# Attention weights turned by vector-engine blocks and DMAs, in place of tensor-engine transposes, for the last eight head pairs

## The chip, the cores and the metric

The kernel runs on one core of a Trainium2 chip. The metric is the device time of one execution in microseconds (us). The engines are TensorE (PE; its weight loads are listed as PEld), VectorE (DVE), ScalarE (ACT), GpSimd (POOL) and SyncE (SP). SP computes nothing here; it issues all the DMAs of the kernel before. Every engine works through its own queue in order, and semaphores tie the queues together.

## The reference, cut to what matters

Four batches of 576 tokens, 8 heads of width 64, all in float32. Three parts follow one another:

```
attention  out_d   = softmax(q_d k_d^T / 8) v_d      q_d, k_d, v_d: means over groups of 4 tokens
           out_loc = softmax(mask(q k^T / 8)) v      mask: |i - j| < 4
           x       = repeat(out_d, 4) + out_loc
block 1    x = x + relu(layernorm(x) w_ch1) w_ch2            512 -> 2048 -> 512
block 2    u = x + (token mixing over 576 -> 256 -> 576 with relu)
           out = u + relu(u w_ch1') w_ch2'                   512 -> 1536 -> 512
```

The change touches the local attention alone (`out_loc`), between the exponential of its scores and their product with v.

## The kernel before, in words

**Attention by pairs.** 4 batches of 4 pairs of heads make 16 pairs, numbered 0 to 15. For a pair, the local scores are computed in 9 blocks of 64 queries against a band of 70 keys (`KW`), which lie in 5 tiles of 128 queries (`NTL`). The steps are functions of the code: `s_pe` (L265 on) computes scores and mask into two PSUM banks, one per head; `s_max` (DVE) takes the row maximum; `s_exp` (L294 on, the ACT instruction is L300) writes the exponentials to the SBUF tile `sm`, with queries on the partitions. `t_pe` (L363) turns each of the 10 tiles (2 heads x 5) by a PE transpose, 128 queries x 70 keys to 70 keys x 128 queries, in three groups that take one PSUM bank each (4, 4 and 2 tiles). `t_copy` (L370) copies each group on ACT to the SBUF tile `et`, with keys on the partitions. `av_pe` (L468) multiplies `et` with v, and `av_norm` divides by the row sum (for pairs 4 to 15 ten small ACT instructions, L502). The coarse attention of the pair (`q_sums`, `d_pe`, `d_max`, `d_exp`, `td_pe`, `td_copy`, `avd_pe`, `avd_norm`) runs beside it, goes through a scratch in HBM (`up_write` L428, `up_read` L439 and L443) and is added into `x` by `av_add` (POOL, L515). `sm` and `et` have one buffer each for pairs 5 to 15, so the transposes of pair n must have read `sm` before pair n+1 writes it, and `av_pe` of pair n-1 must have read `et` before pair n fills it.

**Block 1 and 2 by units.** Tokens go in 9 chunks of 256. A unit is one chunk with 128 hidden columns: `g1` (L629, 12 matmuls of 256 columns into a PSUM bank of `h`), then relu and a split into a high and a low part, on ACT (L635, high) and DVE (L636, low), into `ht`, then `g2` (L650, 6 matmuls of 512 columns that accumulate the chunk's output). There are 16 units a chunk in block 1 and 12 in block 2, 252 in all. In the program's order, `g1` of unit i+1 stands ahead of `g2` of unit i. Weights of block 1 arrive by SP in 32 pieces of 512 KB (`load_unit`, L190). The last 28 of them pass through the staging tile `st` (`stage`, L140 on, 3 buffers of 1024 words a partition); five steps turn a piece to two float32r parts: three on DVE (L149, L154, L159), one on ACT (L164), one on DVE (L167). At most three pieces are loaded and not yet converted.

**The order of work.** Pairs 0 to 4 follow a list written out by hand (`START`). From there each step gets a position in the row of units (`put`): the pairs' steps are spread by `LATER` over units 1 to 25, 26 to 51 and 52 to 82, one step every 1.0 to 1.4 units, in the order `a_scores(n)`, `a_values_down(n-1)`, `a_down(n)`, `a_values(n-1)`, `a_turn(n)`, `a_turn_down(n)`. `a_scores(8)` has position 20.2, `a_down(8)` 22.6, `a_values(7)` 23.8 and `a_turn(8)` 26; one piece of weights is split in each of the units 0 to 27, and three ahead of it is loaded. A scheduler of the compiler then places the instructions by a plan of time; the position is an instruction's priority in it. The queue of each engine is fixed when the kernel is built.

**A turn of the same kind that is there already.** For chunks 3 to 17, the normalized or mixed tokens are turned by `xt_turn`: a DVE instruction transposes each 32x32 block of 128x512 in place (L579), and 16 DMAs of 16 KB, issued by SP (L586), bring each block row to its partitions in runs of 128 bytes.

Of the kernel before, what the change touches and what calls it, by code (L numbers as in the profile page):

```python
# [7 lines left out]
F32 = mybir.dt.float32  # L8
F32R = mybir.dt.float32r
I32 = mybir.dt.int32  # L10
ACTF = mybir.ActivationFunctionType
# [15 lines left out]
KW = 70  # L27
NTL = 5
# [11 lines left out]
SETS = 3  # L40

EARLY = 2

START = """
    q_sums 0; s_pe 0; s_max 0; fill; d_pe 0; q_sums 1; s_exp 0; d_max 0; fill; fill; fill; v_sums 0;
# [46 lines left out]
def block_kernel(ctx: ExitStack, tc: tile.TileContext, qk, vw, vg, g_ln, wa, t1, t2, wb, band, out):  # L92
    nc = tc.nc
    UA = wa.shape[0]
    UB = wb.shape[0]
    scale = 1.0 / float(D) ** 0.5
# [28 lines left out]
    def psg(tag=None):  # L125
        if tag is None:
            turn[0] += 1
            tag = rota[turn[0] % len(rota)]
        return POOLS[tag].tile([128, 512], F32, tag=tag, name=tag)
# [10 lines left out]
    def stage(n):  # L140
        return sp["pool"].tile([128, 2 * QW], I32, tag="st", name="st", bufs=sp["n"])[:, :2 * n]
# [36 lines left out]
    def load_unit(i, part, gate=None):  # L178
        w, m = (wa, i) if i < UA else (wb, i - UA)
        if i < EARLY:  # L180
            if part == 0:
# [39 lines left out]
    def buf(n, tag):  # L221
        if n == SETS and tag == "qk":
            return extra[-1][tag]
        if n < START_PAIRS and n % SETS:
            return extra[n % SETS - 1][tag]
        return at.tile([128, WORDS[tag]], F32, tag=tag, name=tag, bufs=1)
# [3 lines left out]
    def att_load(n, tag):  # L230
        if n < len(order):
            b, p = order[n]
            src = {"qk": qk, "vw": vw, "vg": vg}[tag][b, p]
            t = buf(n, tag)
            nc.sync.dma_start(out=t[:src.shape[0]], in_=src)
            ld[n, tag] = t
# [10 lines left out]
    sts = {}  # L247
# [45 lines left out]

    def s_exp(n):  # L294
        nm = nms[n]
        sm = sts[n]["sm"] = buf(n, "sm").rearrange("p (h t k) -> p h t k", h=2, t=NTL)
        pss = pending.pop((n, "s"))
        for h in range(2):
            for tl in range(NTL):
                nc.scalar.activation(  # L300
                    out=sm[:, h, tl], in_=pss[h][:, tl], func=ACTF.Exp, scale=scale, bias=nm[:, h, tl]
                )

    def a_scores(n):
        for f in (q_sums, s_pe, s_max, s_exp):
            f(n)

    def d_pe(n, tag=None):
        qkd = sts[n].pop("qkd")
        pss = []  # L310
        for h in range(2):
            ps = psg(tag)
            psv = ps[:HG, :2 * SG].rearrange("q (c k) -> q c k", c=2)
            pss.append(psv)
        for c in range(2):
            for h in range(2):
                d = slice(64 * h, 64 * h + 64)
                nc.tensor.matmul(  # L318
                    out=pss[h][:, c, :], lhsT=qkd[d, 0, c * HG:(c + 1) * HG], rhs=qkd[d, 1, :],
                    start=True, stop=True,  # L320
                )
        ld.pop((n, "qk"))
        pending[n, "d"] = pss
# [17 lines left out]
    def v_sums(n):  # L341
        vgt = ld[n, "vg"][:HG].rearrange("p (c n) -> p c n", c=2)
        vd = sts[n]["vd"] = vgt[:, :, :130].rearrange("p c (h d) -> p c h d", h=2)
        for t in range(3):
# [3 lines left out]
                in1=vgt[:, :, o:o + 128].rearrange("p c (h d) -> p c h d", h=2), op=ALU.add,  # L348
            )

    def a_down(n):
        d_pe(n)
        att_load(ahead(n), "qk")
        for f in (d_max, d_exp, v_sums):
            f(n)
# [171 lines left out]
    def ahead(n):  # L527
        return n + 1 if n >= START_PAIRS else len(order)
# [246 lines left out]
    def put(pos, f, *args):  # L775
        u, half = divmod(int(2 * pos), 2)
        u = min(u, NSEQ - 1)
        (bg if half else mid)[u].append(lambda: f(*args))
# [84 lines left out]
    def conv_step(k):  # L863
# [5 lines left out]

    steps = {f.__name__: f for f in (  # L870
        q_sums, v_sums, s_max, s_exp, d_max, d_exp, t_pe, t_copy, td_pe, td_copy, avd_pe, avd_norm, up_write,
        up_read, av_pe, av_norm, load, fill, consts, ln_center, xt_pe, xt_hi, xt_lo,
    )}
# [4 lines left out]
    with tc.manual_schedule():  # L878
# [17 lines left out]
        rota[:] = ["acc", "g"]  # L896
        nl[0] = nsp[0] = EARLY * NPC
        for step in START.split(";"):
# [15 lines left out]
    for n in range(START_PAIRS, len(order) + 1):  # L914
        a = [(f, n) for f in (a_scores, a_down, a_turn, a_turn_down)] if n < len(order) else []
        v = [(f, n - 1) for f in (a_values_down, a_values)] if n > START_PAIRS else []
        later += a[:1] + v[:1] + a[1:2] + v[1:] + a[2:]
    o = 0
    for i, (u0, u1) in enumerate(LATER):
        e = later.index((a_values, NP * (i + 2) - 1)) + 1  # L920
        for k, (f, n) in enumerate(later[o:e]):
            put(u0 + k * (u1 - u0) / (e - o), f, n)
        o = e
    for c in range(2, NCH):
        put_prep1(c, base[c] - 1)
# [122 lines left out]
```

## Time and profile before

| | |
|---|---|
| three runs | 948.16, 951.56, 956.02 us; median 951.56 |
| the profiled execution | 952.27 us, of which 950.5 us are the span of the program's instructions |
| mean granted TensorE clock | 0.989 of full speed |
| busy in the span | PE 916.2 us, PEld 801.0, DVE 447.9, ACT 280.6, POOL 147.5 |
| packets of the DMA queue | 113,040 |

Times in the trace are counted from the start of the span. A group of instructions is one line of the code on one engine with one kind of operands; "mean" is the mean duration of one. Matmuls overlap, so that their durations add up to more than the time they take; the chain of waits shows what each adds. Instructions that issue DMAs are not counted as busy time.

### The profile page before, as it was taken

To read this page: it belongs to the slowest core of one execution; us is meant where nothing else is said; L and a number is where in the kernel's file an instruction comes from. 1 tells how busy PE (TensorE), PEld (TensorE's weight loads), DVE (VectorE), ACT (ScalarE), POOL (GpSimd) and SP (SyncE) were. 2 spreads that over 40 slices of the span, in tenths; PEclk is the share of its full clock that TensorE was granted. 3 is DMA by queue.
4 is the path that set the end of the run, shared out by engine and by line. 5 is a ranking of instruction groups with operands and counts; after the bars stand their busy time and mean duration, and the time that the engine had idled before them with its cause. 6 is when DMAs were issued, how large, how long until landed. Compare 5 with 4: busy or idle time off the path is not lost.

```text
span 950.5 us, 17304 instructions
## 1 busy us (share of the span) xinstructions
PE 916.2 (96%) x6702; PEld 801.0 (84%) x6702; DVE 447.9 (47%) x1044; ACT 280.6 (30%) x809; POOL 147.5 (16%) x176
## 2 busy tenths in 40 slices
PE   7879999899999999999999999999999999999998
PEld 5667878778888888888889988787888888999997
DVE  4785788794225252276312267896322322222211
ACT  5444344344443343323111122332112111111111
POOL 6443214213322221111010000111001000000000
PEclk9888999999999999999999999999999999999999
DMA  8653565534232132234212025663212211110100
GB/s 221 183 188 115 157 194 182 169 104 106 83 105 67 47 104 62 67 106 144 73 28 63 23 83 150 190 187 111 57 44 63 51 36 33 45 35 13 44 23 23
DMA packets 113121, 89.78 MB, mean 94 GB/s; under 512 B 73264, under 2 KB 91952, under 8 KB 113040
## 3 DMA queue, kind: packets, MB, share of 16 engines
q1 hardware_dynamic: 113040, 88.68, 32.7%
q8 instruction: 53, 0.87, 0.4%
q14 instruction: 28, 0.23, 0.1%
HBM read 66.62 MB, written 14.16 MB: 85 GB/s over the span
## 4 chain that ended last, share of the span: by engine, by line
PE 78%; DVE 8%; DMA 8%; SPq 2%; ACT 1%; issue 1%; POOL 1%; DVEq 0%; ACTq 0%
PE h L629 33%; PE acc L650 31%; DMA up_scr<-od 2%; DMA st<-in_wb_dram 2%; PE k L650 2%; PE k L729 2%; SPq L586 2%; DMA xr<-x_scr 2%; DVE cv L159 2%; PE g L760 2%; DVE cv L154 1%; PE g L282 1%; PE g L363 1%; PE g L318 1%; PE g L468 1%
## 5 line engine op out<-in xcount | busy, mean ns | idle before, releaser
L629 PEld LDWEIGHTS h<-xt,w 128*128 128x128 f32 x3024 | 395.5, 190 | 25.0 <-ACT w L164 1.9
L629 PE MATMUL h<-xt,w 128*128 128x256 f32 x3024 | 411.8, 284 | 1.6 <-ACT w L164 1.0
L650 PE MATMUL acc<-w,ht 128*128 128x512 f32 x1416 | 378.7, 399 | 8.1 <-ACT ht L635 3.6
L650 PEld LDWEIGHTS acc<-w,ht 128*128 128x128 f32 x1416 | 252.2, 189 | 61.5 <-ACT ht L635 5.7
L636 DVE SCALAR_TENSOR_TENSOR ht<-h,ht 128x256 fp32r<-128x256 f32 x252 | 105.8, 421 | 354.6 <-ACT ht L635 354.3
L635 ACT ACTIVATE ht<-h 128x256 fp32r<-128x256 f32 x252 | 96.4, 383 | 394.0 <-PE h L629 370.4
L714 POOL TENSOR_TENSOR xs<-xr,xs 128x512 fp32r<-128x512 f32 x20 | 26.6, 1330 | 292.4 <-ACT xs L713 292.4
L164 ACT ACTIVATE w<-cv 128x512 fp32r<-128x512 f32 x56 | 35.5, 635 | 70.7 <-DVE cv L159 70.5
L346 POOL TENSOR_TENSOR vg<-vg 72x256 f32<-72x256 f32 x39 | 32.8, 841 | 144.7 <-DMA vg<-in_vg_dram 143.5
L167 DVE TENSOR_TENSOR w<-cv,w 128x512 fp32r<-128x512 f32 x56 | 42.6, 764 | 6.4 <-ACT w L164 6.2
L159 DVE SCALAR_TENSOR_TENSOR cv<-st,cv 128x512 int32<-128x512 int32 (+4 forms) x63 | 42.8, 684 | 0.6
L154 DVE SCALAR_TENSOR_TENSOR cv<-st,cv 128x512 int32<-128x512 int32 (+4 forms) x63 | 42.4, 677 | 0.7
L515 POOL TENSOR_TENSOR x<-x,pt 128x256 f32<-128x256 f32 (+2 forms) x44 | 28.0, 649 | 80.2 <-DMA x<-up_scr 47.9
L729 PE MATMUL k<-xs,t1w 128*128 128x512 f32 (+1 forms) x120 | 33.5, 410 | 2.2 <-ACT xs L713 1.4
L760 PE MATMUL g<-r,t2w 128*128 128x512 f32 x120 | 34.0, 395 | 0.0
L593 ACT ACTIVATE xt<-xt 128x512 fp32r<-128x512 f32 x30 | 19.0, 632 | 50.0 <-DMA xt<-xc 49.9
L149 DVE TENSOR_SCALAR cv<-st 128x512 int32<-128x512 int32 (+4 forms) x63 | 25.8, 412 | 13.8 <-DMA st<-in_wb_dram 8.9
L594 DVE TENSOR_TENSOR xt<-xt 128x512 fp32r<-128x512 f32 x30 | 20.6, 686 | 23.6 <-ACT xt L593 23.5
L650 PE MATMUL k<-w,ht 128*128 128x512 f32 x96 | 27.6, 409 | 0.1
L729 PEld LDWEIGHTS k<-xs,t1w 128*128 128x128 f32 (+1 forms) x120 | 19.1, 188 | 7.2 <-ACT xs L713 2.1
L502 ACT ACTIVATE pt<-g,rz 128x64 f32<-128x64 f32 (+1 forms) x78 | 17.4, 322 | 23.2 <-DVE rz L492 21.8
L760 PEld LDWEIGHTS g<-r,t2w 128*128 128x128 f32 x120 | 20.9, 189 | 3.0
(160 smaller groups left out, 700.6 us busy)
## 6 DMA issues: line engine op xcount, KB each, us to landing
st<-in_wa_dram SPq DMA_DIRECT2D x28, 512.0 KB
st<-in_wb_dram SPq DMA_DIRECT2D x24, 512.0 KB
xt<-xc SPq DMA_DIRECT2D x480, 16.0 KB
qk<-in_qk_dram SPq DMA_DIRECT2D x13, 579.0 KB
x_scr<-x SPq DMA_DIRECT2D x18, 256.0 KB
x<-x_scr SPq DMA_DIRECT2D x9, 512.0 KB
out_dram<-x SPq DMA_DIRECT2D x18, 256.0 KB
vw<-in_vw_dram SPq DMA_DIRECT2D x13, 319.9 KB
```

Source lines behind the costliest of these rows:

```text
L154: nc.vector.scalar_tensor_tensor(out=f, in0=h, scalar=-0x40000000, in1=f, op0=ALU.bitwise_and, op1=ALU.bitwise_or)
L159: nc.vector.scalar_tensor_tensor(out=f, in0=l, scalar=29, in1=f, op0=ALU.logical_shift_right, op1=ALU.bitwise_or)
L164: nc.scalar.activation(out=hi, in_=f.bitcast(F32), func=ACTF.Copy)
L167: nc.vector.tensor_tensor(out=lo, in0=f.bitcast(F32), in1=f32(hi), op=ALU.subtract)
L346: nc.gpsimd.tensor_tensor(out=vd[:, :, :, :D], in0=vd[:, :, :, :D], in1=vgt[:, :, o:o + 128].rearrange("p c (h d) -> p c h d", h=2), op=AL ...
L515: (eng or nc.gpsimd).tensor_tensor(out=x, in0=x, in1=tmp[rows, tl:tl + k].rearrange("p t h d -> p t (h d)"), op=ALU.add)
L629: nc.tensor.matmul(out=hp[:, :CN], lhsT=w[:, 0, a, kk * 128:(kk + 1) * 128], rhs=xT[c][:, kk, e, :], start=(n == 0), stop=(n == 3 * KD - 1),)
L635: nc.scalar.activation(out=t[:, 0], in_=hp[:, :CN], func=ACTF.Relu)
L636: nc.vector.scalar_tensor_tensor(out=t[:, 1], in0=hp[:, :CN], scalar=0.0, in1=f32(t[:, 0]), op0=ALU.max, op1=ALU.subtract)
L650: nc.tensor.matmul(out=acc[c, j], lhsT=t[:, a, j * 128:(j + 1) * 128], rhs=w[:, 1, e, :], start=(m == 0 and n == 0), stop=(last and n == 2),)
L729: nc.tensor.matmul(out=rps[b, m], lhsT=tokw["t1"][rows, a, n, m * 128:(m + 1) * 128], rhs=t[rows, e, :], start=(n == 0 and i == 0), stop=( ...
L760: nc.tensor.matmul(out=ps, lhsT=tokw["t2"][:, a, m, o:o + 128], rhs=r_t[b][:, m, e, :], start=(i == 0), stop=(i == len(ops) - 1),)
```

## The change

For pairs 8 to 15 (`TURNED`), the exponentials go to a tile of `stage`, with each tile of 70 keys padded to 96 (`KB`) and the pad set to zero by POOL. In `a_down`, DVE transposes the 32x32 blocks of the 128x960 tile in place (`a_blocks`). Where `a_turn` stood, 12 DMAs on ACT's queue (`a_bring`) bring the blocks to `et`: for each of 4 groups of 32 queries and 3 groups of keys (32, 32 and 6), 10 runs of 128 bytes on each partition. That is 320, 320 and 60 runs, 40, 40 and 7.5 KB. They are put two at a time, every half unit. `t_pe` and `t_copy` fall away for these pairs. Pairs 0 to 7 stay as they are.

```diff
+TURNED = 8
+KB = 96
...
     def s_exp(n):
         nm = nms[n]
-        sm = sts[n]["sm"] = buf(n, "sm").rearrange("p (h t k) -> p h t k", h=2, t=NTL)
+        if n < TURNED:
+            sm = sts[n]["sm"] = buf(n, "sm").rearrange("p (h t k) -> p h t k", h=2, t=NTL)
+        else:
+
+            sm = sts[n]["sm"] = stage(NTL * KB).bitcast(F32).rearrange("p (h t k) -> p h t k", h=2, t=NTL)
+            nc.gpsimd.memset(sm[:, :, :, KW:], 0.0)
         pss = pending.pop((n, "s"))
         for h in range(2):
             for tl in range(NTL):
                 nc.scalar.activation(
-                    out=sm[:, h, tl], in_=pss[h][:, tl], func=ACTF.Exp, scale=scale, bias=nm[:, h, tl]
+                    out=sm[:, h, tl, :KW], in_=pss[h][:, tl], func=ACTF.Exp, scale=scale, bias=nm[:, h, tl]
                 )
...
+    def a_blocks(n):
+
+        sm = sts[n]["sm"].rearrange("p h t k -> p (h t k)")
+        nc.vector.transpose(out=sm, in_=sm)
+
+    def a_bring(n, jb, i):
+        if (jb, i) == (0, 0):
+            sts[n]["et"] = buf(n, "et")[:KW]
+        k = min(32, KW - 32 * jb)
+        src = sts[n]["sm"].rearrange("p h t (j b) -> p (h t) j b", b=32)
+        dst = sts[n]["et"].rearrange("p (t q) -> p t q", t=2 * NTL)
+        nc.scalar.dma_start(
+            out=dst[32 * jb:32 * jb + k, :, 32 * i:32 * i + 32], in_=src[32 * i:32 * i + k, :, jb, :]
+        )
+
     def a_down(n):
+        if n >= TURNED:
+            a_blocks(n)
         d_pe(n)
...
         for k, (f, n) in enumerate(later[o:e]):
-            put(u0 + k * (u1 - u0) / (e - o), f, n)
+            u = u0 + k * (u1 - u0) / (e - o)
+            if f is a_turn and n >= TURNED:
+                for x in range(12):
+                    put(u + x // 2 * 0.5, a_bring, n, *divmod(x, 4))
+            else:
+                put(u, f, n)
```

## Rows read from the trace of the kernel before

**Rows 1.** Page: busy time of the engines; busy tenths of PE in 40 slices.
```profile
PE 916.2 (96%) x6702; PEld 801.0 (84%) x6702; DVE 447.9 (47%) x1044; ACT 280.6 (30%) x809; POOL 147.5 (16%) x176
PE   7879999899999999999999999999999999999998
```
**Rows 2.** Windows: stretch, busy us (instructions) of PE, PEld, DVE, ACT, POOL; PE clock, DMA share, GB/s.
```profile
175.00:200.00 25.00, 20.99 (x160) 17.30 (x159) 21.70 (x43) 11.21 (x33) 9.82 (x10) 1.00 0.39 126
...
250.00:275.00 25.00, 25.00 (x266) 21.86 (x265) 6.02 (x20) 9.73 (x35) 6.44 (x10) 1.00 0.27 75
...
375.00:400.00 25.00, 25.00 (x214) 22.14 (x212) 6.29 (x19) 8.06 (x26) 1.92 (x3) 1.00 0.20 55
```
**Rows 3.** Windows: 190 to 402 us in one stretch, the same columns.
```profile
190.00:402.00 212.00, 210.15 (x1860) 183.12 (x1859) 90.25 (x251) 82.75 (x285) 46.39 (x68) 1.00 0.30 83
```
**Rows 4.** Chain of waits, 384 to 390 us: start, us, what.
```profile
384.93 0.44 PE g L363 x4
385.37 0.44 PE k L363 x4
385.81 0.22 PE g L363 x2
386.02 1.43 PE h L629 x12
387.46 1.39 PE acc L650 x6
```
**Rows 5.** Groups by shape, 190 to 402 us: count, busy us, mean ns, idle before.
```profile
L635 ACT ACTIVATE ht<-h 128x256 fp32r<-128x256 f32 x54 | 20.9, 389 | 55.3 <-PE h L629 51.4 <-PE k L650 3.1 <-DVE xc L546 0.4
...
L363 PE MATMUL g<-ident,sm 128*70 128x128 f32 x52 | 8.5, 273 | 0.2 <-ACT pt L502 0.2
...
L370 ACT ACTIVATE et<-g 70x512 f32<-70x512 f32 x9 | 5.2, 586 | 1.9 <-PE g L363 1.9
...
L579 DVE STREAM_TRANSPOSE xc<-xc 128x512 f32<-128x512 f32 x7 | 4.9, 700 | 0.0
...
L363 PE MATMUL k<-ident,sm 128*70 128x128 f32 x28 | 4.2, 274 | 0.0
L370 ACT ACTIVATE et<-k 70x512 f32<-70x512 f32 x7 | 4.1, 587 | 2.0 <-PE g L468 2.0
...
L370 ACT ACTIVATE et<-g 70x256 f32<-70x256 f32 x8 | 3.0, 376 | 4.0 <-PE g L363 4.0
```
**Rows 6.** By line, the whole span: durations of SP's DMA issues in ns, min/median/max.
```profile
L586 SPq DMA_DIRECT2D xt<-xc x480: 585/599/1564, 205.8 to 899.0; - x160
L428 SPq DMA_DIRECT2D up_scr<-od x26: 786/827/932, 19.3 to 396.5; - x26
```
**Rows 7.** DMA view, 580.5 to 587 us: queue, packets, MB, share of 16 engines.
```profile
q1 hardware_dynamic: 1296, 0.66, 40.1%
```
**Rows 8.** Page, groups: POOL's additions into x.
```profile
L515 POOL TENSOR_TENSOR x<-x,pt 128x256 f32<-128x256 f32 (+2 forms) x44 | 28.0, 649 | 80.2 <-DMA x<-up_scr 47.9
```
**Rows 9.** Timelines of ACT, SP and PE, 169 to 188 us: start, us, what.
```profile
169.41 2.21 ACT L300 ACTIVATE sm<-g,nm 128x70 f32<-128x70 f32 x10 [2.86 <-DVE nm L292]
...
171.13 0.33 SPq L190 DMA_DIRECT2D st<-in_wa_dram  x1
...
179.66 7.51 SPq L190 DMA_DIRECT2D st<-in_wa_dram  x4
...
182.66 1.39 PE L468 MATMUL g<-vw,et 70*64 70x65 f32 x36
```
**Rows 10.** Chain of waits, 170 to 200 us: start, us, what.
```profile
179.66 4.77 DMA st<-in_wa_dram
184.46 0.43 DVE cv L149
184.88 0.60 DVE cv L159
...
192.67 0.62 DVE cv L159
193.29 0.13 issue
193.42 0.96 DVE w L167
194.38 0.04 issue
194.43 0.74 PE acc L650 x2
```

## Prediction

> **What bounds the kernel now.** The page comes first [rows 1]: PE is busy for 96% of the span and no other engine for half of it, so the question is where PE is not the bound. The slices of PE stand at 9 from about a quarter of the span on and lower ahead of it. The windows [rows 2] make that sharper. From 250 us on PE is busy 25.00 of 25 us, while ACT is busy 8 to 10 and DVE about 6. From 175 to 200 us PE has 20.99 and DVE 21.70 of 25: there the last weight pieces of block 1 are being converted, and that chain is the bound. The chain of waits for this stretch [rows 10] shows it: a piece's DMA (4.77 us on the chain), the DVE steps, and then PE's `g2` waiting for the converted piece at 194.43.
>
> The stretch that the change touches is 190 to 402 us, in which all 80 transposes of pairs 8 to 15 lie (52 + 28 in [rows 5]). PE is busy 210.15 of its 212 us [rows 3]. So for pairs 9 to 15 a microsecond of PE work taken away is a microsecond of the time, as long as nothing new makes PE wait; for pair 8, whose turn lies in the weight stretch, it is not.
>
> **What is removed.** The transposes last 273 and 274 ns each [rows 5], but they overlap. The chain shows what they add [rows 4]: 0.44 + 0.44 + 0.22 = 1.10 us for ten, and by starts slightly less, since the durations of neighbours differ. I take 1.05 us for a pair. Pairs 9 to 15: 7 x 1.05 = 7.4 us. Pair 8: nothing counted, 1.05 at best.
>
> The Trainium skill ("TensorE: Matmul & The Clock Gate", Part 4: PE-mode transpose) gives about 275 ns for a transpose in one kernel's context; the duration in [rows 5] agrees. Read as time taken from PE it would be 80 x 0.275 = 22 us by estimate, and the change would be worth over 2%. The chain contradicts that reading: ten of them move PE on by 1.10 us, not 2.75.
>
> ACT loses three copies a pair: 586 + 587 + 376 ns [rows 5] = 1.55 us, or about 12 us over eight pairs. ACT is busy 82.75 of 212 us [rows 3], so this is worth nothing by itself. Three PSUM banks a pair are no longer taken; PE has only 212 - 210.15 = 1.85 us without work [rows 3], so there is little for that to give after 190 us.
>
> **What is added on DVE.** One block transpose of 128x960 a pair. The nearest row is 700 ns for 128x512 [rows 5], so 960 / 512 x 0.70 = 1.31 us. After 200 us it lies in DVE's idle time. DVE's one duty toward PE is the low half of `ht`: from the end of a `g1`, PE has one `g2` and one `g1` to do (1.39 + 1.43 = 2.82 us, [rows 4]) before it needs that half, and ACT's half takes 0.39 [rows 5]. A block of 1.31 us fits into that. For pair 8 DVE is on the chain: +1.3 us (0 to 1.3).
>
> POOL gets a memset of 260 values on each partition; the nearest row is an addition at 649 ns [rows 8]. POOL is busy for 46 of 212 us [rows 3] and nothing on PE's chain hangs on it: 0, and no more than 0.65 a pair where it delays an addition.
>
> **What is added on ACT.** 12 DMA issues a pair. No DMA is issued by ACT in this trace, so the price p of an issue on ACT is bounded by SP's rows [rows 6]: 0.60 us for 128 runs of 128 bytes (the same kind of transfer), 0.83 us for 288 runs of 512 bytes. A price that grew with the runs would give 0.60 x 320 / 128 = 1.5 us; the second row speaks against that (2.25 times the runs, 1.4 times the time). Its size puts a bring between the two: I take 0.7, with 0.6 and 1.5 as ends. Then ACT gets 12 x 0.7 = 8.4 us a pair and loses 1.55. All that ACT has to do in 212 us becomes 82.75 + 8 x 6.9 = 138 us: still far from full.
>
> What stands behind a bring is the relu (L635), on which PE's `g2` waits. The brings are put over three units, 11.8 us at the pace of this stretch (212 us [rows 3] for 54 relus [rows 5] is 3.93 us a unit). In these ACT has 12p, three relus (1.2 us) and the two copies of `td_copy` (0.7 by the smaller of the copies in [rows 5]). With p = 0.7 that is 10.3 of 11.8: dense, and it fits. On top a relu may be 2.82 - 0.39 = 2.4 us late before PE feels it. So PE begins to wait when 12p + 1.9 exceeds 11.8 + 2.4 = 14.2, at p of about 1.02. Below that I count 0.1 us a pair, 0.7 for seven; ends are 0 and, at p = 1.5, 18 + 1.9 - 14.2 = 5.7 us a pair.
>
> A bring also waits for the DVE transpose (two steps earlier in the row of units) and for `av_pe` of the pair before to have read `et` (one step earlier); t_copy had that second wait already.
>
> **DMA traffic.** A pair adds 4 x (320 + 320 + 60) = 2,800 runs. The stretch in [rows 7] holds little but such traffic: 0.401 x 16 x 6.5 us / 1,296 packets is 32 ns each, with some 4 KB packets among them, so that is an upper end. 2,800 x 32 ns / 16 = at most 5.6 us of each DMA engine a pair, of 26 us on average (212 / 8), where the share is now 0.20 to 0.41 [rows 2, 3]. It fits; `av_pe` comes five steps after the first bring. Cost 0.
>
> **The staging tile.** `sm` of pairs 8 to 15 takes one of three `stage` buffers. Pairs 9 to 15 have them to themselves, since the last weight piece is loaded at 187 us [rows 9]. Pair 8 does not. Its exponentials run at 169.4 us, when three loaded pieces fill all three buffers, and the load at 171.13 goes out as soon as one is free [rows 9]. Now either that load or the exponentials wait, and the remaining five loads share two buffers until the brings of pair 8 have read theirs. With two buffers a piece's load (4.77) and conversion (0.43, then two steps of about 0.6) [rows 10] still come to about 3.2 us a piece, while the pace now is 12 us for four pieces (179.66 to about 192, the last but one being converted). So two buffers nearly keep up: +1 us. If instead a load is tied to the very buffer of pair 8, which is read out at about 195 us at the earliest (`av_pe` of pair 7 ends at about 184 [rows 9], and the brings follow it for about 10 us), up to 11 us are lost; if the order of SP's queue changes for the better, about 1 is won.
>
> **The sum.** -7.4 + 1.3 (DVE, pair 8) + 1.0 (staging) + 0.7 (relus) = -4.4 us. From the profiled execution, 952.27, that leads to 947.9; it lies 0.7 above the median of the runs, so against 951.56 the forecast is 947.2, rounded to 947.0: 0.5% faster.
>
> **Rivals.**
>
> *ACT's queue holds back the relus.* The price of an issue decides: nothing below 1.02 us, all of the gain gone at 1.02 + 4.4 / 8 / 12 = 1.07, and over 1% slower (14 us of stalls, 1.75 a pair) from 1.17. At 1.3 us the stalls are 12 x 0.28 x 8 = 27 us and the time 974. For it: the issues of SP reach 1.56 us at times [rows 6], the runs are 2.5 times as many as in the first row, and ACT has a relu to serve in every unit. Against it: both medians lie below 1.02, and a third of the brings have a fifth of the runs. Chance 0.14.
>
> *The staging buffer stalls the weights.* Up to 11 us in place of 1: 957, between 950 and 961. For it: the stretch is bound by these very pieces [rows 10]. Against it: the brings may run as soon as their inputs are there, and the other two buffers turn over meanwhile. Chance 0.14.
>
> *More is won than the transposes.* Ahead of 200 us PE is idle for 25 - 20.99 = 4.0 us [rows 2], some of it around pair 8, whose turn shares two PSUM banks with all the small steps; if the staging costs nothing and half of this and pair 8's 1.05 come back: 952.3 - 7.4 - 1.05 - 2 - 0.7 = 941. Chance 0.17. If each transpose cost PE its whole duration, 0.27 us, 80 would give 22 us and 930; the chain speaks against it: 0.02.
>
> *The forecast*, 943 to 951: 0.53.
>
> **How the numbers follow.** A change of 1%, 9.5 us, is about what a measurement of this kernel can tell from none: under 942.0 is faster, over 961.1 slower. Faster: 0.02, most of the rival at 941 (0.12) and a tail of the forecast (0.07), 0.21. Slower: the ACT rival above 1.17 us (0.12) and a tail of the staging one (0.04), 0.16. Within: 0.63. The range that leaves out two in ten reaches from 938 (the rival at 941 with a margin) to 963 (the staging rival and a little of ACT's).
>
> **What would show it.** In the profile after: 80 PE transposes, 24 copies and their PSUM banks gone, 8 block transposes of about 1.3 us, 96 DMA issues on ACT of about 0.7 us. Right, if the same units take about 1 us less of PE per pair between 200 and 400 us and PE stays full there. The price on ACT is wrong if `g2` waits for L635 in the units after a bring, or if an issue lasts about 1 us or more. The staging step is wrong if the loads of the last pieces wait on SP for L159 or for a bring beyond 190 us. The forecast as a whole fails if the gain per pair after 250 us is not about 1 us, or if the units ahead of 200 us shift by more than 5 us.

## The result and the profile after

The changed kernel takes 959.73 us (median of 7 runs, 957.75 to 961.49), against 951.74 us for the kernel before in 7 runs (948.16 to 956.02). The ratio is 1.0083, with a 95% interval of 1.0061 to 1.0104: slower by 0.8%, or 7.9 us. The forecast was 0.5% faster. The profiled execution of the changed kernel took 957.75 us, with a span of 956.0 us. It is the fastest of the seven, at a mean granted clock of 0.987; the mean of the seven is 0.983.

In the changed kernel `g1` is L654, `g2` L675, the relu L660 (ACT) and L661 (DVE), the mask and the products of the scores L276 and L285, the block transpose L362, the bring L370, `td_copy` L415, `avd_pe` L432 and `av_pe` L493. The page gives PE's busy time and the queue that ACT now issues to (packets, MB, share of 16 engines), which answer to [rows 1]:

```profile
PE 916.4 (96%) x6622; PEld 797.0 (83%) x6622; DVE 454.7 (48%) x1052; ACT 270.2 (28%) x785; POOL 152.2 (16%) x184
...
q10 hardware_dynamic: 23616, 2.87, 2.0%
```

The 80 transposes are gone (6,702 to 6,622 instructions), and yet PE is busy for as long as before: what is left takes longer. The windows of the changed kernel, with the columns of [rows 2, 3], say where:

```profile
175.00:200.00 25.00, 21.42 (x145) 17.45 (x144) 19.95 (x42) 9.59 (x27) 10.27 (x11) 0.91 0.60 156
250.00:275.00 25.00, 25.00 (x238) 21.47 (x237) 9.07 (x22) 9.87 (x36) 6.78 (x11) 1.00 0.38 93
375.00:400.00 25.00, 25.00 (x194) 22.15 (x194) 5.87 (x16) 8.15 (x29) 3.82 (x6) 1.00 0.27 62
...
190.00:402.00 212.00, 205.54 (x1723) 175.96 (x1722) 95.40 (x254) 72.17 (x258) 48.59 (x75) 0.98 0.39 95
```

From 250 us on PE is full, as it was. But between 190 and 402 us it now lies idle for 6.5 us in place of 1.85, and its granted clock is 0.98 there, where it was 1.00; from 175 to 200 us it is 0.91, where it was 1.00 [rows 2]. The waits of PE in that stretch (engine, line, what it waited for, us in total, times, longest) of the changed kernel:

```profile
PE k L432 <- ACT pt L415: 2.7, 1, 2.7
PE acc L675 <- DVE w L170: 1.0, 1, 1.0
PE g L326 <- DVE rd L442: 0.9, 1, 0.9
PE h L654 <- DVE w L170: 0.8, 1, 0.8
PE g L598 <- ACT st L308: 0.7, 1, 0.7
PE acc L675 <- ACT ht L660: 0.4, 1, 0.4
```

The relu (L660), on which the prediction looked, costs 0.4 us. The longest wait is for `pt`, which `td_copy` writes, and it is a single one. In the kernel before, the longest of this list is the same wait, with 0.5 us. The line of the bring shows its issues (ns, min/median/max) and who stood behind it on ACT:

```profile
L370 ACTq DMA_DIRECT2D et<-st x96: 592/636/1615, 187.9 to 392.4; - x96
...
  ACT ht L660: 11.4, 3
  ACT pt L415: 10.3, 2
```

An issue costs 0.64 us by the median, near the 0.7 of the prediction. The chain of waits from 226 to 239 us (start, us, what) shows what the single wait is made of:

```profile
226.70 3.77 DMA vw<-in_vw_dram
...
230.49 0.59 ACTq L370
...
231.12 0.80 ACTq L370
...
232.03 0.41 ACT pt L415
...
232.49 1.42 PE k L432 x16
233.91 1.02 PE g L326 x4
234.93 2.75 PE acc L675 x6
237.68 1.42 PE h L654 x12
```

The brings of pair 9 come up on ACT. One of them is held until the load of v (SP, 320 KB, sent at 226.70 us, behind turns on SP's queue) has landed at 230.47 us. It does not read that load. In the trace the transfers of both queues count their completions on eight semaphores in turn, the load and this bring have the same one, and that semaphore is the one that the issue waits for. Behind it stands `td_copy`, whose result PE wants next. PE is without work from 229.8 to 232.5 us, and it pays a second time: the six `g2` matmuls at 234.93 us take 2.75 us, where six took 1.39 [rows 4]. Windows of 1 us with PE's busy time, its granted clock, the DMA share and GB/s:

```profile
230.00:231.00 1.00, 0.00 (x0) 1.00 0.31 55
231.00:232.00 1.00, 0.00 (x0) 1.00 0.21 31
...
234.00:235.00 1.00, 1.00 (x5) 0.51 1.01 348
235.00:236.00 1.00, 1.00 (x3) 0.50 1.17 219
236.00:237.00 1.00, 1.00 (x4) 0.50 0.57 193
237.00:238.00 1.00, 1.00 (x7) 0.79 0.59 147
```

About 1.5 us after PE has work again, the granted clock falls from 2.4 to 1.2 GHz for about 3.4 us, in which PE is busy: 0.49 + 0.50 + 0.50 + 0.21 = 1.7 us more. Over all runs the mean granted clock is 0.983, against 0.987 before (mean of the 11 runs of the kernel before that ran beside the first experiments).

The second loss is in the score products. The timeline of PE for pair 12 (start, us, what), first in the kernel before, where 36 matmuls (two for each of the 18 products of the code) follow two masks:

```profile
273.51 0.33 PE L273 MATMUL k<-maskr,identr 128*128 128x350 f32 x1
273.68 0.32 PE L273 MATMUL g<-maskr,identr 128*128 128x350 f32 x1
273.93 0.27 PE L282 MATMUL k<-qk 64*64 64x70 f32 x1
273.93 0.27 PE L282 MATMUL g<-qk 64*64 64x70 f32 x1
...
274.70 1.70 PE L629 MATMUL h<-xt,w 128*128 128x256 f32 x12
```

and then in the changed kernel:

```profile
273.45 0.40 PE L276 MATMUL k<-maskr,identr 128*128 128x350 f32 x1
273.79 0.45 PE L285 MATMUL k<-qk 64*64 64x70 f32 x6
274.17 0.43 PE L276 MATMUL g<-maskr,identr 128*128 128x350 f32 x1
274.53 0.33 PE L285 MATMUL g<-qk 64*64 64x70 f32 x2
274.79 1.19 PE L675 MATMUL acc<-w,ht 128*128 128x512 f32 x4
275.91 0.33 PE L285 MATMUL g<-qk 64*64 64x70 f32 x2
276.18 0.73 PE L675 MATMUL acc<-w,ht 128*128 128x512 f32 x2
...
279.65 0.27 PE L285 MATMUL g<-qk 64*64 64x70 f32 x1
279.65 0.27 PE L285 MATMUL k<-qk 64*64 64x70 f32 x1
...
280.29 1.70 PE L654 MATMUL h<-xt,w 128*128 128x256 f32 x12
```

Before, the two heads (banks `k` and `g`) take turns: their products start within 0.01 us of each other and run side by side, 36 of them in 274.70 - 273.93 = 0.77 us, and the whole step moves PE on by 274.70 - 273.51 = 1.19 us. Afterwards six matmuls of one head alone take 0.38 us (273.79 to 274.17), and the step is cut up by `g2`: (274.79 - 273.45) + (276.18 - 275.91) + (280.29 - 279.65) = 2.25 us. The order on PE is fixed when the kernel is built. The change took other work out of that order, and in the new order the score products stand elsewhere. The Trainium skill ("TensorE: Matmul & The Clock Gate", section "Why this matters for your kernels") says that matmuls with small contractions which lie in different row groups run at the same time; the starts of the two heads within 0.01 us agree, where the heads alternate.

### The profile page after: what moved, and what is told of

Read it like the earlier page. It is cut to its first block, busy times and chain, and to the rows that moved or that the text cites. A ratio compares the mean times of both kernels' runs of the same rounds, so it can differ in the third digit from the quotient of the medians.

```text
span 956.0 us, 17285 instructions
## 1 busy us (share of the span) xinstructions
PE 916.4 (96%) x6622; PEld 797.0 (83%) x6622; DVE 454.7 (48%) x1052; ACT 270.2 (28%) x785; POOL 152.2 (16%) x184
## 4 chain that ended last, share of the span: by engine, by line
PE 77%; DVE 9%; DMA 8%; SPq 3%; ACT 1%; issue 1%; POOL 0%; ACTq 0%; DVEq 0%
PE h L654 33%; PE acc L675 31%; DMA st<-in_wb_dram 3%; DVE cv L162 2%; PE k L754 2%; DVE cv L157 2%; PE k L675 2%; DMA up_scr<-od 2%; PE g L785 2%; SPq L611 1%; PE g L285 1%; DMA xr<-x_scr 1%; DMA st<-in_wa_dram 1%; DVE cv L152 1%; DVE w L170 1%
## 5 line engine op out<-in xcount | busy, mean ns | idle before, releaser
L654 PEld LDWEIGHTS h<-xt,w 128*128 128x128 f32 x3024 | 398.8, 192 | 27.9 <-DVE w L170 2.3
L654 PE MATMUL h<-xt,w 128*128 128x256 f32 x3024 | 413.6, 285 | 2.5 <-DVE w L170 1.4
L675 PE MATMUL acc<-w,ht 128*128 128x512 f32 x1416 | 380.1, 400 | 6.1 <-DVE w L170 2.4
L675 PEld LDWEIGHTS acc<-w,ht 128*128 128x128 f32 x1416 | 253.0, 190 | 59.6 <-DVE w L170 4.1
L661 DVE SCALAR_TENSOR_TENSOR ht<-h,ht 128x256 fp32r<-128x256 f32 x252 | 105.8, 421 | 339.7 <-ACT ht L660 339.0
L660 ACT ACTIVATE ht<-h 128x256 fp32r<-128x256 f32 x252 | 96.4, 383 | 420.8 <-PE h L654 382.2
L162 DVE SCALAR_TENSOR_TENSOR cv<-st,cv 128x512 int32<-128x512 int32 (+4 forms) x63 | 42.8, 685 | 0.6
L675 PE MATMUL k<-w,ht 128*128 128x512 f32 x96 | 27.7, 406 | 0.2 <-ACT ht L660 0.2
L604 DVE STREAM_TRANSPOSE xc<-x 128x512 f32<-128x512 f32 x18 | 12.8, 710 | 20.1 <-DMA xt<-xc 19.8
```

The costliest lines, as they stand in the source:

```text
L162: nc.vector.scalar_tensor_tensor(out=f, in0=l, scalar=29, in1=f, op0=ALU.logical_shift_right, op1=ALU.bitwise_or)
L654: nc.tensor.matmul(out=hp[:, :CN], lhsT=w[:, 0, a, kk * 128:(kk + 1) * 128], rhs=xT[c][:, kk, e, :], start=(n == 0), stop=(n == 3 * KD - 1),)
L660: nc.scalar.activation(out=t[:, 0], in_=hp[:, :CN], func=ACTF.Relu)
L661: nc.vector.scalar_tensor_tensor(out=t[:, 1], in0=hp[:, :CN], scalar=0.0, in1=f32(t[:, 0]), op0=ALU.max, op1=ALU.subtract)
L675: nc.tensor.matmul(out=acc[c, j], lhsT=t[:, a, j * 128:(j + 1) * 128], rhs=w[:, 1, e, :], start=(m == 0 and n == 0), stop=(last and n == 2),)
```

## Experiments

Every kernel below ran in 5 rounds beside the kernel before. "Excess" is the ratio, less one, of 951.5 us; the intervals are 1 to 3 us to either side.

| run | median us | before | ratio, 95% interval | excess us | mean granted clock |
|---|---|---|---|---|---|
| the changed kernel | 959.73 | 951.74 | 1.0083 (1.0061 to 1.0104) | +7.9 | 0.983 |
| e1_sp | 960.37 | 951.43 | 1.0094 (1.0077 to 1.0112) | +8.9 | 0.983 |
| e4_t9 | 958.39 | 951.43 | 1.0080 (1.0065 to 1.0096) | +7.6 | 0.984 |
| e6_pool | 969.96 | 951.43 | 1.0203 (1.0179 to 1.0226) | +19.3 | 0.978 |
| e7_halves | 977.15 | 951.43 | 1.0286 (1.0257 to 1.0315) | +27.2 | 0.975 |
| e8_vw | 959.66 | 950.98 | 1.0101 (1.0082 to 1.0120) | +9.6 | 0.983 |
| e9_hp | 957.41 | 950.98 | 1.0073 (1.0050 to 1.0096) | +6.9 | 0.983 |
| e10_before_hp | 954.09 | 950.98 | 1.0027 (1.0013 to 1.0041) | +2.6 | 0.988 |
| e11_dve | 960.15 | 950.98 | 1.0098 (1.0081 to 1.0115) | +9.3 | 0.983 |
| e16_whole | 955.00 | 951.13 | 1.0033 (1.0014 to 1.0052) | +3.1 | 0.983 |
| e18_before_whole | 949.53 | 951.13 | 0.9987 (0.9965 to 1.0008) | -1.2 | 0.987 |
| e21_dve_t9 | 949.20 | 951.13 | 0.9977 (0.9956 to 0.9997) | -2.2 | 0.988 |
| e19_dve_t9_whole | 946.04 | 951.13 | 0.9939 (0.9916 to 0.9963) | -5.8 | 0.987 |
| e20_t9_whole | 953.79 | 951.80 | 1.0015 (0.9993 to 1.0037) | +1.4 | 0.984 |
| e22_late | 946.90 | 951.80 | 0.9939 (0.9915 to 0.9962) | -5.8 | 0.988 |
| e23_idle | 960.48 | 951.80 | 1.0086 (1.0055 to 1.0117) | +8.2 | 0.979 |
| e24_idle_here | 947.94 | 951.55 | 0.9935 (0.9911 to 0.9959) | -6.2 | 0.987 |
| e25_late9 | 947.50 | 951.55 | 0.9956 (0.9937 to 0.9974) | -4.2 | 0.987 |
| e26_after_late | 955.00 | 951.55 | 1.0024 (1.0004 to 1.0045) | +2.3 | 0.985 |

### Who issues the brings, and how many issues there are

The first theories were ACT (the issues in its queue), STAGING (pair 8 among the weight pieces) and TRAFFIC (the DMA engines). Three runs change the issues.

e1_sp and e6_pool, brings issued by SP or by POOL:

```diff
-        nc.scalar.dma_start(
+        nc.sync.dma_start(
```

> The changed kernel (959.7 us against 951.7) with its 96 bring DMAs issued by SP in place of ACT; all else the same. Theory ACT (the brings stand in ACT's queue ahead of relus and small copies, PE waits or is filled with small pieces): with ACT free, pairs 9 to 15 give the 1 us a pair that the transposes cost, only the loss in the weight stretch stays: about 950 to 953. Theory STAGING (pair 8's tile among the weight pieces is the whole loss): no better than 958. Theory TRAFFIC (the runs of 128 bytes or the block transposes on DVE slow the rest): 958 to 961.

> The changed kernel with the 96 brings issued by POOL in place of ACT. Theory ACT: as with SP, 950 to 954, as long as POOL's own sums and additions are not late. Theory STAGING: 958 or more. Theory TRAFFIC: 958 to 961.

e7_halves, each bring as two of half the size:

```diff
-        nc.scalar.dma_start(
-            out=dst[32 * jb:32 * jb + k, :, 32 * i:32 * i + 32], in_=src[32 * i:32 * i + k, :, jb, :]
-        )
+        for o in (0, NTL):
+            nc.scalar.dma_start(
+                out=dst[32 * jb:32 * jb + k, o:o + NTL, 32 * i:32 * i + 32],
+                in_=src[32 * i:32 * i + k, o:o + NTL, jb, :],
+            )
```

> The changed kernel with each bring cut into two DMAs of half the runs (24 issues a pair on ACT, the same bytes and the same runs). Theory ACT: ACT's issue time goes from 66 us to about 120 us in the stretch of eight pairs, and the loss per pair grows: 965 to 985. Theory STAGING: at most 2 us more, 960 to 962. Theory TRAFFIC: no change, 958 to 961.

Measured: 960.4, 970.0 and 977.2 us. TRAFFIC falls: with the same bytes and runs, 96 more issues cost 17 us more. But ACT's queue is not the whole answer either, since on SP the same brings cost as much. In the trace of e1_sp PE's waits for ACT's and DVE's halves of `ht` come to 2.5 and 3.5 us; that these come from turns and loads that the brings make late on SP is argued, not tested. The 970.0 us on POOL lie outside what any of the three theories gave. In that trace PE lies idle for 9.8 us between 200 and 402 us, in many waits of at most 2.2 us, and no run takes them apart. That something which PE needs stands behind the brings on each of the three queues fits the runs, but it is shown for ACT alone, further down. The Trainium skill ("DMA: Bandwidth & Descriptors", section "Issuing engines are not separate DMA queues") says that a second issuing engine saves only the sequencer's time; e1_sp does not contradict it: 960.4 us with all DMAs on SP, 959.7 with SP and ACT.

### Pair 8 in the weight stretch

e4_t9:

```diff
-TURNED = 8
+TURNED = 9
```

> The changed kernel with pair 8 left to PE (TURNED = 9), so that no tile of the new kind lies among the weight pieces. Theory STAGING: the 4 to 8 us that are lost between units 23 and 37 come back: 952 to 955. Theory ACT: one pair of eight less, about 1 us better: 958 to 959. Theory TRAFFIC: likewise about 958.7.

958.4 us, 1.3 less than the changed kernel; from e16_whole to e20_t9_whole, which differ in the same way, it is 1.2. By the ratios these are 0.3 and 1.7 us, and neither is clear of its interval: the net cost of pair 8, its ten transposes included, is small.

The trace of the changed kernel shows what STAGING does. From PE's waits between 145 and 200 us, and from ACT's timeline:

```profile
PE g L432 <- POOL st L304: 1.4, 1, 1.4
...
169.45 2.20 ACT L308 ACTIVATE st<-g,nm 128x70 f32<-128x70 f32 x10 [4.63 <-DVE cv L162]
```

The exponentials of pair 8 have their row maxima at 167.58 us and start at 169.45, when DVE's L162 has freed a staging buffer. POOL's memset waits for the same buffer. PE's wait stands under the memset, which had ended at 169.79; it ended at 170.67, 0.06 us after ACT had signalled the fifth exponential, the last that reads the first head's scores. So the exponentials wait 1.9 us, PE 1.4 us behind them, and from 172 to 176 us the granted clock is 0.57 (1.00 before). The same wait of 1.4 us stands in the traces of e16_whole and e26_after_late, and not in those of e4_t9 and e20_t9_whole.

### The load of v

e8_vw moved the load of v of pairs 9 to 15 from `a_values` to `a_turn_down`, in the code behind the brings:

```diff
     def a_turn_down(n):
+        if n > TURNED:
+            att_load(n, "vw")
...
-        att_load(ahead(n), "vw")
+        if ahead(n) < TURNED + 1:
+            att_load(ahead(n), "vw")
```

> Edit: for pairs 9 to 15 the 320 KB load of v is issued with the step that runs the block transposes of the next pair, no longer right in front of the 12 brings. LANDING (an issue on ACT stands still until an earlier transfer, which counts on the same semaphore, has landed; the long load of v just before the brings is the worst of these): the waits of 1.7 to 2.0 us in the chain behind that load go, and the time comes to 954 to 957 us, 3 to 6 below the changed kernel's 959.7. PIECES (what is lost is lost by small steps of the scores being cut into more pieces on PE): no change, 959 to 960. PRICE (12 issues of 0.69 us a pair in ACT's queue, whatever they wait for): no change, 959 to 960.

959.7 us. The run does not answer its question: the planner sent the load only 1 us earlier (225.75 us), and a bring waited for it as before. Its chain reads:

```profile
225.75 3.89 DMA vw<-in_vw_dram
...
229.66 0.59 ACTq L370
```

### The score products

e9_hp and its control e10_before_hp gave the score products of pairs 9 to 15 a higher priority:

```diff
-        for f in (q_sums, s_pe, s_max, s_exp):
-            f(n)
+        q_sums(n)
+        with tc.high_priority(offset=200 if n > TURNED else 0):
+            s_pe(n)
+        s_max(n)
+        s_exp(n)
```

> Edit: the score products of pairs 9 to 15 get a higher priority in the planner, so that each pair's stand together on PE again (20 pieces in the whole program in place of 31; the kernel before has 22). PIECES: every further break costs PE about 0.25 us and some masking, 3.4 to 4.6 us in all; they come back, and the time is 955 to 956. LANDING and PRICE: the pieces only fill places where PE would wait for ACT anyway, so PE waits there instead, and the time stays at 958 to 961.

> Edit: the same priority in the kernel before, whose score products lie in 22 pieces with and without it. All theories: no change, 950 to 953 us. If it is faster by more than 2 us, the gain of the run with the priority in the changed kernel says nothing of the change.

The first won only 2 us (1.0 by the ratios), and the control lost 3, which no theory had expected. The count of pieces was the wrong measure. With the priority the products of one head go out as soon as its bank is free, and those of the other head follow: fewer pieces, but the heads no longer run beside each other. By the steps from one start to the next, the masks and products of pairs 11 to 15 take 6.1 us of PE in the kernel before and 9.8 in the control, in seven stretches each. So the next pair of runs holds both banks first. The mask of the bank that comes free last goes ahead, everything else is issued behind it, and the heads alternate:

```diff
+        pss = [psg(tag)[:, :NTL * KW] for h in range(2)]
+        with tc.high_priority(offset=200 if n > 8 else 0):
+            last = nc.tensor.matmul(out=pss[1], lhsT=identr, rhs=..., start=True, stop=False)
+            with tc.issue_after(last.ins) if n > 8 else ExitStack():
+                nc.tensor.matmul(out=pss[0], lhsT=identr, rhs=..., start=True, stop=False)
...
```

> Edit: the changed kernel, with the 38 score products of each pair from 9 on kept in one block on PE, the two heads in turn (first the mask of the bank that comes free last, the rest behind it). SPLIT (a third of the loss and more: in the changed kernel these products of pairs 11 to 15 are cut up and their heads no longer overlap, 10.4 us in place of 6.1 by the steps from one start to the next): 4 us come back, 955 to 956 us; the granted clock stays at 0.983. QUEUE AND CLOCK (the rest: PE waits for ACT, whose queue the brings hold, and runs at half the clock for some us behind each such wait): the cuts only fill waits, so 958 to 960. Both may hold at once: then 955 to 956 with the clock still at 0.983.

> Edit: the same block for pairs 9 to 15 in the kernel before, whose products of pairs 11 to 15 stand together already but for one cut. Control. SPLIT: 950 to 952 us, at most 1 us won. If it wins as much as the run with the block in the changed kernel, the change did not cost that part.

955.0 us: 4.7 come back, and the clock stays at 0.983. The control wins 1.6 (its interval includes no change). So some 3 to 4 us of the loss are the change's split of these products, and the rest lies elsewhere. The traces agree: by the steps from one start to the next, the masks and products of pairs 11 to 15 take 10.4 us in the changed kernel, 6.3 in e16_whole and 6.1 in e18_before_whole.

### Without any DMA

e11_dve turns the blocks by 12 DVE instructions a pair, from `stage` straight to the rows of `et` where they belong, with no DMA and no issue:

```diff
-        nc.scalar.dma_start(
-            out=dst[32 * jb:32 * jb + k, :, 32 * i:32 * i + 32], in_=src[32 * i:32 * i + k, :, jb, :]
-        )
+        nc.vector.transpose(out=dst[32 * jb:32 * jb + 32, :, 32 * i:32 * i + 32], in_=src[32 * i:32 * i + 32, :, jb, :])
...
-        if n >= TURNED:
-            a_blocks(n)
```

> Edit: no DMA and no issue on ACT: for pairs 8 to 15 twelve block transposes on DVE a pair read the staged exponentials and write each 32-row block straight to its keys. PE's transposes stay gone. PRICE and LANDING (both say that the loss lies in ACT's queue): the loss of the changed kernel goes; PE keeps the 7.4 us of the transposes less what a busier DVE costs, 12 steps of an estimated 0.4 to 0.5 us a pair against one of 1.18, so 943 to 949 us. PIECES: part of it, 948 to 954. If the staging buffers or the missing PSUM copies were the cause, it stays near 958.

A miss: 960.2 us. Each of the 12 takes 0.50 us, so pair 8 puts 6 us on DVE in the weight stretch, which DVE's conversions bound, and PE waits for DVE there. The line of these instructions (ns, min/median/max):

```profile
L369 DVE STREAM_TRANSPOSE et<-st x96: 489/502/506, 190.1 to 398.7; 32x320 f32<-32x320 f32 x96
```

and from PE's waits between 185 and 215 us in the same kernel:

```profile
PE k L670 <- DVE ht L656: 5.3, 1, 5.3
```

e21_dve_t9 is the same with `TURNED = 9`, and e19_dve_t9_whole has the block of score products as well.

> Edit: the twelve block transposes on DVE in place of the DMAs, and only for pairs 9 to 15: pair 8 keeps PE and its own buffer, so nothing is added to the stretch in which weight pieces are converted. QUEUE AND CLOCK: no bring holds ACT and no stall at pair 8, so the granted clock is back at 0.987 and the stretch up to 250 us costs nothing more; what stays is the split score products (4 us lost) against 7 pairs x 1.05 won: 947 to 950 us. If the queue was not the cause, it stays above 955.

> Edit: as the run before it (DVE, pairs 9 to 15), and the score products of these pairs in one block. SPLIT and QUEUE AND CLOCK together: both losses are gone and the 7.4 us of the transposes are left, 943 to 946 us, less than the kernel before. SPLIT alone wrong: as the run before it, 947 to 950.

949.2 and 946.0 us, as expected (the second at the edge), with the clock back at 0.988 and 0.987. So with DVE in place of the DMAs and the block both losses are gone, and e19_dve_t9_whole beats the kernel before by 0.6%. Against e4_t9, which turns the same pairs by DMAs on ACT, e21_dve_t9 is 9.2 us faster; with the block on both sides (e20_t9_whole, below, against e19_dve_t9_whole) it is 7.8. That is what the brings on ACT's queue cost over DVE's steps.

### What it is about a bring on ACT's queue

e20_t9_whole is the base: the changed kernel with `TURNED = 9` and the block. e22_late starts all brings one unit later, e25_late9 those of pair 9 alone, and e26_after_late all of them in the changed kernel itself:

```diff
-                    put(u + x // 2 * 0.5, a_bring, n, *divmod(x, 4))
+                    put(u + 1 + x // 2 * 0.5, a_bring, n, *divmod(x, 4))
```

(e25_late9 has `u + (n == 9) + ...`.) e23_idle and e24_idle_here start from the DVE version and add 84 issues of tiny DMAs that wait for no data; in e24 each is held to its place in ACT's program:

```diff
+        tc.keep_in_program_order(nc.scalar.dma_start(out=idle[:, 4 * jb + i], in_=ident[:, 2 * i:2 * i + 2]))
```

> Edit: the changed kernel with pair 8 left on PE and the score products of pairs 9 to 15 in one block; the brings stay DMAs on ACT's queue. The parts measured so far add up to 959.7 - 1.3 (pair 8) - 4.7 (block) = 953.7: 953 to 955 us. If parts overlap, 955 to 957. Its distance to the version with DVE in place of the brings (946.0) is what the brings on ACT cost, 7 to 8 us.

> Edit: as e20_t9_whole, and the 12 brings of a pair start one unit (about 3.9 us) later, so that the products of the pair before have read the buffer when the first bring comes up on ACT. DATA WAIT: waits of 2.0 to 2.6 us ahead of the first bring of 4 to 5 pairs go, with them PE's stalls behind them: 948 to 951 us. PRICE: 12 issues of 0.69 us a pair stand in the queue as before: 953 to 955, as e20_t9_whole.

> Edit: the DVE version with one block of score products (946.0), and beside each of the twelve DVE steps of a pair a DMA of 128 x 8 bytes issued by ACT, from a constant to a spare tile: it waits for no data and nothing waits for it (84 issues). PRICE: the issues hold the relus back as the brings do, 952 to 956 us. DATA WAIT: 946 to 948.

> Edit: as e23_idle (the DVE version, 946.0, with 84 issues on ACT of DMAs that wait for no data), but each issue is held to its place in ACT's program, among the relus where the brings stand. PRICE: 12 issues of 0.55 to 0.65 us a pair cost what the brings cost, 952 to 954 us. WAITS (what costs is that the queue stands while a bring waits for its data or for a transfer): 946 to 948 us.

> Edit: as e20_t9_whole (953.8), and only the brings of pair 9 start one unit later; those of pairs 10 to 15 stay. ONE PLACE (a single stall of about 3 us of PE at some 226 us, with the half clock behind it): nearly all of what moving every pair won comes back, 947 to 949 us. EVERY PAIR: a seventh of 6.9 us, 952 to 953.

> Edit: the changed kernel itself (pair 8 included, score products as planned), with the brings of all pairs one unit later and nothing else. If the parts add up: 959.7 - 6.9 = 952.8, so 952 to 954 us, a little slower than the kernel before. If pair 8 in the weight stretch now sets the stall: 956 to 960.

e20_t9_whole: 953.8 us, so the parts add up. e22_late: 946.9, 6.9 us less (7.2 by the ratios) and more than its theory gave. e25_late9: 947.5, 6.3 less (5.6), so most of it is won by one pair. e26_after_late: 955.0, 4.7 less than the changed kernel (5.6), between the two ranges expected. e23_idle: 960.5, a miss of the test, since the planner put the issues, which nothing held, at the start of the program, where they cost 10 us before the first unit. e24_idle_here: 947.9, within 2 us of the same kernel without the issues, and no slower by the ratios. Its issues are as long as the brings' (ns, min/median/max):

```profile
L374 ACTq DMA_DIRECT2D idle<-ident x84: 472/612/1472, 217.8 to 393.9; - x84
```

So twelve issues of 0.61 us a pair in ACT's queue cost little by themselves. At 246.8 us four of them hold even `td_copy` up, for 2.4 us, and in the list of PE's waits none for `td_copy` follows. What costs is one place, where the queue stands and something that PE wants at once is behind it. ACT's timelines at pair 9 show the difference. e20_t9_whole (L373 the bring, L418 `td_copy`, in brackets the idle time before and what ended it):

```profile
223.31 5.51 ACTq L373 DMA_DIRECT2D et<-st  x4
228.93 0.41 ACT L418 ACTIVATE pt<-g 72x288 f32<-72x288 f32 x1 [5.73 <-DMA et<-st]
```

e25_late9:

```profile
221.48 0.41 ACT L418 ACTIVATE pt<-g 72x288 f32<-72x288 f32 x1 [0.98 <-POOL x L543]
221.78 0.40 ACT L418 ACTIVATE pt<-k 72x288 f32<-72x288 f32 x1
222.32 0.60 ACTq L373 DMA_DIRECT2D et<-st  x1
...
224.83 2.24 ACTq L373 DMA_DIRECT2D et<-st  x3
```

One unit later, `td_copy` stands ahead of the waiting brings in place of behind them, and PE's wait of 3.0 us for `pt` is gone. It was not the bring's own data that decided, as the expectation of e22_late had it: the waits ahead of the brings (time without work or issue on ACT just before one, where it is over 0.15 us) add up to 17.3 us in e20_t9_whole, 15.9 in e22_late and 18.5 in e25_late9. In the late ones they only hold back other instructions.

The traces place the gain. From the first `g1` matmul of unit 36 to that of unit 40 (units counted from 0, 12 matmuls into `h` each), e20_t9_whole takes 24.8 us, e25_late9 20.0, e22_late 18.3 and the kernel before 20.0. The fall of the clock becomes shorter, but it does not go. Windows of PE in e20_t9_whole (the first two lines) and in e25_late9, where the next window is at 1.00 again:

```profile
230.00:235.00 5.00, 5.00 (x26) 0.59 0.78 221
235.00:240.00 5.00, 5.00 (x30) 0.72 0.38 100
...
230.00:235.00 5.00, 4.52 (x18) 0.66 0.56 145
```

In half-clock time that is 6.9 us against 3.4. Between 200 and 402 us PE's idle time falls from 5.4 us to 3.7 in e25_late9 and 3.3 in e22_late, since other waits are left; in e25_late9 the longest is 1.4 us, for `ht`. The mean granted clock over the runs is 0.984 in e20_t9_whole and 0.987 to 0.988 in the two late ones, and 0.0035 of 953 us is about 3 us. So of the 6 to 7 us about 2 are PE's idle time and 2 (by these traces) to 3 (by the means) are clock; the rest the traces do not name.

## Why the prediction was wrong, point by point

- **What bounds the kernel** was right: PE does, from 200 us on, and each microsecond of PE counted, the ones added too.
- **The transposes** were sized right. From one start to the next, the 60 of pairs 10 to 15 held PE for 6.05 us, 1.01 for ten; the prediction took 1.05. That the whole 7.4 us can be had is not shown: from e18_before_whole to e19_dve_t9_whole 3.5 us are won (4.6 by the ratios), with an interval of some 3 us to either side.
- **The block transpose on DVE**: 1.31 us predicted, 1.18 measured. In e25_late9 one such block stands ahead of the low half of `ht`, and PE waits 0.5 us for it (231.5 us); in the changed kernel PE has no such wait. **POOL's memset**: 0.32 us, and the one wait of PE under its name is that for pair 8's exponentials. **DMA traffic** at no cost: e7_halves has the same traffic and 17 us more, so traffic was not it.
- **Pair 8 in the weight stretch**: 1.3 + 1.0 us predicted, 1.2 to 1.3 measured by the medians (0.3 to 1.7 by the ratios); the rival with 957 us by this cause is out. That the load or the exponentials would wait for a buffer was right: it was the exponentials. That PE waits behind them for 1.4 us, with a lower clock after it, was not foreseen.
- **The price of an issue**: 0.7 predicted, 0.64 by the median. The rival on ACT's queue hung on this price alone ("nothing below 1.02 us"), and so did the term of 0.7 us for the relus.
- **This step failed.** It weighed how much ACT has to do in three units against how long they last, as if the queue only had to keep up. Twelve issues without waits do keep up, as e24_idle_here shows. But a bring can stand, for the products of the pair before or for a transfer that shares its semaphore, and then everything behind it stands. The prediction named the first of these waits, set it aside because `t_copy` had it already, and did not ask what would be queued behind it. It asked how late the relu may be, which has 2.4 us of slack; `td_copy` it counted as 0.7 us of ACT's time, and not as something that PE wants at once. In its place the runs show a wait of PE of 2.7 us at pair 9 and a lower clock after it. Moving the brings by one unit wins 5.6 to 7.2 us by the ratios, where 0.7 was predicted for the queue.
- **A term was missing**, put at nothing without a reason: that the planner would order PE's other work anew. The split of the score products of pairs 11 to 15 cost 3 to 5 us (4.8 by the changed kernel and e16_whole, less 1.2 for the control). The prediction took the 212 us for the same row of instructions less the transposes.
- **The sum.** 947.0 with these three terms put right: 947.0 + (6.3 - 0.7) + 3.6 - (2.3 - 1.3) = 955.2, against 959.7. Of the 4.5 us left, 1.6 (by the ratios, e25_late9 against e19_dve_t9_whole) lie with the brings that remain after pair 9 is moved; the rest, the distance between the 7.1 us of transposes and the 4.6 that the DVE version wins on its control, stays open within the intervals.

## What to carry to other kernels

Before work is put on an engine's queue, list what stands behind it there and when the bound engine wants each of these, and do so for waits and not only for durations: a DMA issue of 0.6 us can hold a queue for 2 us. Where a planner fixes the order, taking instructions away moves others; compare the order of the bound engine before and after, and look whether operations that overlapped in pairs still do. A single stall of the bound engine can cost its length again in clock, so look for the longest wait and not only for the sum. It need not: in the kernel before PE waits 1.76 us up to 186.47 us, and the granted clock stays at 1.00.

## What was not expected of the hardware

- After PE had been without work for 2.7 us, the granted clock was at half for about 3.4 us, although PE was busy again, and six `g2` took 2.75 us in place of 1.39. After 1.4 us without work at 169 to 171 us it fell too, and after 1.76 us in the kernel before it did not.
- A DMA issue on ACT waited for a transfer that SP had sent and that it has nothing to do with (3.77 us after that was sent): the two share a completion semaphore.
- Score matmuls of one head alone cost PE 0.063 us each where six stood together (0.38 us) and 0.042 where 18 did (0.75 us at 201.86 us in the changed kernel), and 0.021 with the two heads in turn (0.77 us for 36).
